# Cluster-match rows turned as 4-byte pairs, three zero matmuls fewer, and one attention block left in its place

## The chip, the cores and the metric

The kernel runs on one core of a Trainium2 chip. The metric is device time in microseconds (us) of one execution. PE is the matmul engine, ACT the engine that evaluates exponentials and other functions, DVE the vector engine, POOL the general-purpose engine, SP the engine that here only issues transfers (DMAs).

## The reference

Attention in which a query sees only the keys of its own cluster, followed by a gated feed-forward layer (FFN). There are 4 batches, 8 heads, 768 tokens, head size 64, and 16 cluster centroids per head.

```
q_n, k_n, c_n = rows of q, k, centroids divided by their norms
q_assign = argmax(q_n . c_n);  k_assign = argmax(k_n . c_n)      # 16 clusters
scores = where(q_assign == k_assign, scale * q k^T, -1e9)
attn = softmax(scores);  x = attn v            # heads side by side: 3072 x 512
out = (sigmoid(x w_gate) * (x w_val)) w_out     # 512 -> 1536 -> 512
```

## The kernel before, in words

**Units.** Two heads make a pair `p` (four pairs); the 768 queries of a head are halved (`qb` 0 and 1). A block is one batch, one query half and one pair. The list `blocks` holds 32 of them, ordered by batch, half, pair, except that line 256 takes the fifth, (batch 0, half 1, pair 0), and inserts it as the second. A block has six steps. A step is two score matmuls (line 911, 128 keys x 384 queries each, into the PSUM tile `sc`, of which there are two), one exponential on ACT over 128x768 (line 930, `es`), and six value matmuls (line 950) that add up in `av`, the only buffer of its kind. After the sixth step DVE takes reciprocals of the sums (line 988) and scales (line 991). The result is transposed into `x`, by a DMA (line 1014) or by PE and a DVE copy (lines 999 and 1010).

**The mask.** Nothing is masked by a select. Each key and each query gets 16 additional rows, a one where the token's cluster is and zeros elsewhere, weighted so that the product of two equal rows adds a large constant, which the bias of the exponential takes off again. The score matmul therefore contracts over 64+16 = 80 rows. The tiles `even` and `odd` hold the two operands (`NM`: k in 0, q in 1) for even and odd 128-token chunks. For query half 0 the q operand is the one in `even`, for half 1 the one in `odd`.

**Making the rows.** PE multiplies centroids and transposed k and q (lines 854, 734 for batch 0; 588 later) into a `ring` buffer: 32 rows (two heads x 16 clusters) by 384 tokens for each of four combinations. DVE then runs four operations: a transpose in 32x32 blocks into `t1`, so that clusters lie along the free dimension (lines 873, 760, 615); a maximum over each 16 (876, 761, 620); a comparison with that maximum, giving fp16 ones and zeros (863, 750, 598); and a transpose back. In batch 0 the way back is `place` (line 663): six transposes of 32x384 per pair, in the order even k and q of the first half, odd k, even k and q of the second half, odd k, each read from `ohf` with an offset of 16 columns where odd is wanted. The odd q rows are copied from the even tile by one DMA of SP (`odd<-even`, issued at line 281). In the other batches the way back is one transpose of 128x384 (line 608) into `oht`, from which eight DMAs of SP copy 16 rows each into `even` and `odd`.

**The FFN.** `feed` starts when all four pairs of a query half are in `x`: twelve times four gate matmuls, four value matmuls (line 1049), a tanh on ACT (1065) and a product on DVE (1076), and then 36 output matmuls (1096), an ACT scaling (1111) and the store.

**Order.** Every piece of work is a task with an engine, an estimated duration, a due time and its dependencies. A list scheduler places each where it can start first by its own estimates (the smaller due time where two are within 0.02 us) and so writes the order of each engine's queue. On the chip each engine follows its queue strictly, and waits where the next one's inputs are missing. So a changed duration or block order moves instructions on all engines. SP's queue holds the loads of k and q (for part of batch 1, and for batches 2 and 3, in quarters of 96 KB), the transposes into `x`, the mask copies and the stores.

**Warming.** Line 305 issues six 128x512 matmuls on zeros at the start. Line 1176 issues six more, behind the transposes of pair 1 and ahead of the first score matmul.

Of the kernel before, what the change touches and what calls it, by code (L numbers as in the profile page):

```python
# [164 lines left out]
def kernel(  # L165
# [38 lines left out]
        "odd": ([96, 2, S], HP), "oht": ([128, S], HP),  # L204
        "ohf": ([128, QB + NCL], HP), "t1": ([128, QB], FP), "mx": ([128, QB // NCL], FP), "oh": ([128, QB], HP),
        "es": ([128, 2, QB], HP), "rr": ([128, 2 * QCH], FP),
# [47 lines left out]

    for at, of in ((1, 4),):
        blocks.insert(at, blocks.pop(of))
    JS = list(range(0, NCH, 2)) + list(range(1, NCH, 2))
# [219 lines left out]
    act_scaled = nc.scalar.mul  # L477

    def dve_scaled(to, of, by):
        nc.vector.tensor_scalar(to, of, by, None, ALU.mult)  # L480

    def prepare(b, grp, due, step, act=(), queues=("SP",), split=False):
# [98 lines left out]
        for half in range(2):  # L581
# [14 lines left out]
            def same(oh=oh, t1=t1, mx=mx):  # L596
                take(oh)
                nc.vector.tensor_tensor(
                    grouped(oh), grouped(t1),
                    mx.tile[:n].unsqueeze(2).to_broadcast([n, QB // NCL, NCL]), ALU.is_equal,  # L600
                )

# [3 lines left out]
            def back(cols=cols, oh=oh, half=half):  # L606
                t = oht.tile if half else take(oht)
                nc.vector.transpose(t[:n, cols], oh.tile[:n])

# [4 lines left out]
            a1 = od.add(  # L614
                "DVE", 0.53, lambda t1=t1, rg=rg: nc.vector.transpose(take(t1)[:n], rg.tile[:n, :QB]),
                [cl], due, acq=[t1], uses=[rg],
# [36 lines left out]
    def place(b, p, ohf, tiles, last, due, alloc, c):  # L653


        ev, od_ = aug[b, p]
        for n_, (e, nm, h) in enumerate(
            ((0, "k", 0), (0, "q", 0), (1, "k", 0), (0, "k", 1), (0, "q", 1), (1, "k", 1))
        ):
            g = tiles.index((nm, h))  # L660
            m = od.add(
                "DVE", 0.6,
                lambda g=g, e=e, nm=nm, h=h: nc.vector.transpose(  # L663
                    aug[b, p][e].tile[64:96, NM[nm], h * QB : (h + 1) * QB],
                    ohf.tile[32 * g : 32 * g + 32, 16 * e : 16 * e + QB],
                ),
                [last, *alloc], due + 0.3 * n_, uses=[ohf, aug[b, p][e]],
            )
            masked[b, p, e, nm, h] = [c[nm, e, h], m]

        m = dma(
            "SP", lambda: od_.tile[64:80, NM["q"], :], lambda: ev.tile[80:96, NM["q"], :], 0.1,
            [masked[b, p, 0, "q", h][1] for h in range(2)] + alloc, due + (20.0 if p else 2.0), uses=[ev, od_],
        )
        for h in range(2):
            masked[b, p, 1, "q", h] = [c["q", 1, h], m]

    def prepare_pair(b, p, due, step, act=("q",), direct=False):
# [66 lines left out]
        def same():  # L745
            if direct:
                nc.vector.memset(take(oh)[:, QB:], 0.0)
            else:
                take(oh)
            nc.vector.tensor_tensor(  # L750
                grouped(oh), grouped(t1),
                mx.tile.unsqueeze(2).to_broadcast([128, QB // NCL, NCL]), ALU.is_equal,
            )

# [4 lines left out]
        for dur, go, acq, uses in (  # L759
            (0.61, lambda: nc.vector.transpose(take(t1), rg.tile[:, :QB]), t1, [rg]),  # L760
            (0.52, lambda: nc.vector.tensor_reduce(take(mx), grouped(t1), AX.X, ALU.max), mx, [t1]),
            (0.67, same, oh, [t1, mx]),
            (0.55, lambda: nc.vector.transpose(take(oht)[:, :QB], oh.tile), oht, [oh]),
        )[: 3 if direct else 4]:
            last = od.add("DVE", dur, go, [last], due, lat=0.0, acq=[acq], uses=uses)
# [24 lines left out]
    def prepare_first(due):  # L790
# [71 lines left out]
        def same():  # L862
            nc.vector.tensor_tensor(
                grouped(ohf), grouped(t1),
                mx.tile.unsqueeze(2).to_broadcast([128, QB // NCL, NCL]), ALU.is_equal,
            )

# [4 lines left out]
        for dur, go, acq, uses in (  # L872
            (0.58, lambda: nc.vector.transpose(take(t1), rg.tile[:, :QB]), t1, [rg]),
            (
                0.55,
                lambda: nc.vector.tensor_reduce(take(mx), grouped(t1), AX.X, ALU.max), mx, [t1],
            ),
            (0.6, same, None, [t1, mx, ohf]),
        ):
# [293 lines left out]
    def zeros_in_between():  # L1173
        ps = take(z_ring)
        for _ in range(6):
            nc.tensor.matmul(out=ps, lhsT=wz[:, 0:128], rhs=wz, start=True, stop=True)
# [38 lines left out]
```

## Time and profile before

| | |
|---|---|
| median of 3 runs | 328.13 us (327.52 to 328.47) |
| the profiled execution's own time | 327.7 us |
| its span | 325.9 us |
| busy: PE, ACT, DVE, POOL | 316.9, 227.8, 153.3, 64.6 us |
| six zero matmuls of line 1176 | 1.46 us, from 9.63 us on |
| first exponential | 11.69 us |
| first FFN matmul | 43.83 us |
| first output matmul of the FFN | 66.91 us |

A PE row's busy time counts each matmul from its start to its modelled end, and these overlap. A step's real pace is the distance between starts: four FFN matmuls of 128x384 take 0.65 us in the chain, so 0.163 us each, though the row says 325 ns. The granted TensorE clock is 1.00 in every stretch.

### The profile page before, as it was taken

The page shows a single profiled execution, that of the slowest core. Times are in us where ns is not written, and L with a number is a line of the kernel's source. Part 1 is how long each engine was busy: PE and PEld are TensorE (multiplying, and loading weights), DVE is VectorE, ACT ScalarE, POOL GpSimd, SP SyncE. Part 2 cuts the span into 40 slices and gives each one's busy share as a digit, 9 for nine tenths or more (in the row PEclk, how much of TensorE's full clock was granted, in tenths as well). Part 3 has the DMA queues.
Part 4 walks back from the last instruction along what each step waited for, and adds up shares of the span by engine and source line. Part 5 has one row for each costly group of instructions (what it writes and reads, how often), then busy time and mean ns, then how long its engine had stood idle before and what let it go on. Part 6 is the DMA issues. An engine that isn't in the chain of part 4 may idle for free.

```text
span 325.9 us, 7307 instructions
## 1 busy us (share of the span) xinstructions
PE 316.9 (97%) x2814; PEld 188.4 (58%) x2814; DVE 153.3 (47%) x332; ACT 227.8 (70%) x329; POOL 64.6 (20%) x109
## 2 busy tenths in 40 slices
PE   7988999999999999999999999999999999999995
PEld 4555756645666556565566555566566655654652
DVE  3989883546336329561264474742033311540430
ACT  5889958866797678776888677687788867332331
POOL 4997442130005313100024115000000000000000
PEclk9999999999999999999999999999999999999999
DMA  6999999736368884212867955210210012001002
GB/s 212 375 212 254 220 253 199 127 67 141 87 110 172 167 172 141 65 27 62 167 109 156 199 107 152 47 39 12 78 46 12 14 29 73 23 2 64 34 0 97
DMA packets 91522, 36.88 MB, mean 113 GB/s; under 512 B 76960, under 2 KB 86688, under 8 KB 91488
## 3 DMA queue, kind: packets, MB, share of 16 engines
q1 hardware_dynamic: 84960, 26.56, 36.3%
q0 software_dynamic: 6096, 9.44, 13.4%
q8 instruction: 22, 0.36, 0.5%
q10 hardware_dynamic: 432, 0.43, 0.4%
q14 instruction: 12, 0.10, 0.1%
HBM read 28.34 MB, written 6.29 MB: 106 GB/s over the span
## 4 chain that ended last, share of the span: by engine, by line
PE 88%; DVE 3%; DMA 3%; ACT 2%; SPq 1%; issue 1%; ACTq 0%; DVEq 0%
PE ring L1049 37%; PE ring L1096 19%; PE sc L911 17%; PE av L950 10%; PE ring L588 3%; ACT es L930 2%; DMA odd<-even 1%; SPq L281 1%; DVE even L663 1%; PE ring L517 1%; DMA cn<-in_centroids_dram 1%; DMA odd<-oht 1%; DVE odd L663 1%; ACT t L701 0%; PE ring L694 0%
## 5 line engine op out<-in xcount | busy, mean ns | idle before, releaser
L930 ACT ACTIVATE es<-sc,nbias 128x768 f16<-128x768 f32 x192 | 170.0, 902 | 45.1 <-PE sc L911 43.0
L1076 DVE SCALAR_TENSOR_TENSOR hT<-gt,ring 128x384 f16<-128x384 f32 x96 | 53.1, 553 | 102.4 <-PE ring L1049 95.6
L1049 PE MATMUL ring<-x,wv 128*128 128x384 f16 x384 | 78.1, 325 | 0.0
L1049 PE MATMUL ring<-x,wg 128*128 128x384 f16 x384 | 78.1, 326 | 0.0
L950 PEld LDWEIGHTS <-es 128*128 128x128 f16 x1152 | 58.3, 97 | 29.2 <-ACT es L930 2.5
L1096 PE MATMUL ring<-wo,hT 128*128 128x512 f16 x288 | 71.2, 379 | 0.0
L1065 ACT ACTIVATE gt<-ring 128x384 f32<-128x384 f32 x96 | 46.7, 487 | 32.1 <-DVE hT L1076 17.5
L950 PE MATMUL av<-vp,es 128*128 128x65 f16 x1152 | 64.9, 193 | 0.7 <-ACT es L930 0.7
L1049 PEld LDWEIGHTS <-wv 128*128 128x128 f16 x384 | 36.1, 97 | 22.8
L1049 PEld LDWEIGHTS <-wg 128*128 128x128 f16 x384 | 35.4, 97 | 22.8 <-issue 1.2
L550 POOL CAST even<-t 128x768 f16<-128x768 f32 x24 | 19.9, 828 | 105.1 <-PE av L950 33.3
L1096 PEld LDWEIGHTS <-hT 128*128 128x128 f16 x288 | 25.7, 98 | 25.5 <-issue 1.9
L911 PE MATMUL sc<-even 80*128 80x384 f16 x96 | 26.0, 326 | 1.3 <-ACT es L930 1.2
L911 PE MATMUL sc<-odd,even 80*128 80x384 f16 x96 | 26.2, 326 | 1.0 <-DMA odd<-even 1.0
L911 PE MATMUL sc<-even,odd 80*128 80x384 f16 x96 | 26.4, 325 | 0.4 <-DMA odd<-oht 0.2
L911 PE MATMUL sc<-odd 80*128 80x384 f16 x96 | 26.5, 325 | 0.0
L1111 ACT ACTIVATE osb<-ring 128x512 f32<-128x512 f32 x24 | 14.3, 597 | 14.3 <-PE ring L1096 13.5
L911 PEld LDWEIGHTS <-even 80*128 80x128 f16 x192 | 17.0, 98 | 12.5 <-issue 2.3
L911 PEld LDWEIGHTS <-odd 80*128 80x128 f16 x192 | 16.7, 99 | 10.2 <-issue 2.4
L453 POOL CAST vp<-nat 128x384 f16<-128x384 f32 x32 | 15.7, 521 | 29.2 <-DMA nat<-in_v_dram 24.3
L988 DVE RECIPROCAL rr<-av 128x6 f32<-128x6 f32 x32 | 6.1, 189 | 32.7 <-PE av L950 32.4
L498 DVE STREAM_TRANSPOSE t<-nat 128x384 f32<-128x384 f32 x40 | 20.7, 549 | 1.1 <-DMA nat<-in_q_dram 1.1
(78 smaller groups left out, 164.4 us busy)
## 6 DMA issues: line engine op xcount, KB each, us to landing
out_dram<-osb SPq DMA_DIRECT2D x24, 256.0 KB, 2.2
nat<-in_v_dram POOLq DMA_DIRECT2D x12, 384.0 KB, 5.2
nat<-in_k_dram SPq DMA_DIRECT2D x40, 96.0 KB, 3.6
nat<-in_q_dram SPq DMA_DIRECT2D x40, 96.0 KB, 3.4
odd<-even SPq DMA_DIRECT2D x12, 192.0 KB, 3.5
nat<-in_k_dram SPq DMA_DIRECT2D x5, 384.0 KB, 5.0
nat<-in_q_dram SPq DMA_DIRECT2D x5, 384.0 KB, 5.5
nat<-in_v_dram SPq DMA_DIRECT2D x4, 384.0 KB, 6.8
```

The source lines that it names most:

```text
L453: lambda e=e: nc.gpsimd.tensor_copy(vps[i % NVP][:, e, :, 0:D], buf.tile[:, e, :, :]),
L498: nc.vector.transpose(t[:, half * QB : (half + 1) * QB].rearrange("p (c x) -> p c x", x=128), blocks_[:, half],)
L550: nc.gpsimd.tensor_copy(t[:, NM[nm], cols], t32[p, nm].tile[:, cols])
L588: nc.tensor.matmul(out=ps[32 * g : 32 * g + 32, :QB], lhsT=cblk[:, 2 * p + half, :], rhs=t32[p, nm].tile[:, cols], start=True, stop=True,)
L911: nc.tensor.matmul(out=ps[:, i, :QB], lhsT=kb.tile[0:80, 0, e * QB + j // 2 * 128 : e * QB + (j // 2 + 1) * 128], rhs=qb_.tile[0:80, 1, e ...
L930: lambda: nc.scalar.activation(take(es), sc.tile[:, :, :QB], AF.Exp, bias=nbias, scale=D ** -0.5 if quarters(b, p) else scale,),
L950: nc.tensor.matmul(out=av.tile[:, g : g + D + 1], lhsT=es.tile[:, i, c * 128 : (c + 1) * 128], rhs=vp[:, e, j, :], start=first and i == 0 ...
L1049: nc.tensor.matmul(out=ps[:, :QB], lhsT=ws[fc // FPG][:, dcc, fc % FPG, :], rhs=xb.tile[:, dcc, :], start=(dcc == 0), stop=(dcc == NDC - 1),)
L1065: lambda rg=rg, gt=gt: nc.scalar.activation(take(gt), rg.tile[:, :QB], AF.Tanh, scale=0.5),
L1076: nc.vector.scalar_tensor_tensor(t[:, fc, :], gt.tile, 1.0, rv.tile[:, :QB], ALU.add, ALU.mult)
L1096: nc.tensor.matmul(out=ps, lhsT=hb.tile[:, fc, tb * 128 : (tb + 1) * 128], rhs=wos[fc // FPG][:, fc % FPG, :], start=(fc == 0), stop=(fc = ...
L1111: "ACT", 0.5, lambda rg=rg, osb=osb: nc.scalar.mul(take(osb), rg.tile, 0.5),
```

## The change

1. The match rows are written in another order. The transpose of the scores reads its input with stride 2, so that even and odd tokens of each 64 come to lie in two blocks of 32; the comparison (`matched`) writes its ones and zeros so that an even and an odd token's fp16 values are neighbours, 4 bytes together. The way back is then a transpose of half as many 4-byte elements (`turn_matches`): 32x192 in place of 32x384 in `place`, 128x192 in place of 128x384 at the former line 608. `ohf` is padded by 32 columns, not 16. The planner's estimates for these are 0.4 and 0.36 in place of 0.6 and 0.53 us.
2. Three zero matmuls ahead of the scores, not six.
3. Block (batch 0, half 1, pair 0) is not moved forward. Batch 0 runs the four pairs of half 0, then the four of half 1.

```
-        "ohf": ([128, QB + NCL], HP), ...
+        "ohf": ([128, QB + 2 * NCL], HP), ...
-    for at, of in ((1, 4),):
-        blocks.insert(at, blocks.pop(of))
+    def turn_scores(to, of):
+        nc.vector.transpose(
+            to.rearrange("p (b s c) -> p b s c", s=2, c=32),
+            of.rearrange("p (b i s) -> p b s i", s=2, i=32),
+        )
+    def matched(to, of, top):
+        nc.vector.tensor_tensor(
+            to.rearrange("p (b x s) -> p b s x", x=32, s=2).rearrange(
+                "p b s (g c) -> p b s g c", c=NCL
+            ),
+            of.rearrange("p (b s g c) -> p b s g c", s=2, g=2, c=NCL),
+            top.rearrange("p (b s g) -> p b s g", s=2, g=2).unsqueeze(4).to_broadcast(
+                [to.shape[0], QB // 64, 2, 2, NCL]
+            ),
+            ALU.is_equal,
+        )
+    def turn_matches(to, of):
+        nc.vector.transpose(to.bitcast(FP), of.bitcast(FP))
...
-                nc.vector.transpose(t[:n, cols], oh.tile[:n])
+                turn_matches(t[:n, cols], oh.tile[:n])
...
-                "DVE", 0.53, back, [a3], due, seq=turned[-1:],
+                "DVE", 0.36, back, [a3], due, seq=turned[-1:],
...
-                "DVE", 0.6,
-                lambda g=g, e=e, nm=nm, h=h: nc.vector.transpose(
+                "DVE", 0.4,
+                lambda g=g, e=e, nm=nm, h=h: turn_matches(
                     aug[b, p][e].tile[64:96, NM[nm], h * QB : (h + 1) * QB],
-                    ohf.tile[32 * g : 32 * g + 32, 16 * e : 16 * e + QB],
+                    ohf.tile[32 * g : 32 * g + 32, 32 * e : 32 * e + QB],
...
-        for _ in range(6):
+        for _ in range(3):
             nc.tensor.matmul(out=ps, lhsT=wz[:, 0:128], rhs=wz, start=True, stop=True)
-        "PE", 0.22 * 6, zeros_in_between, [], 1.0, seq=[last_turn[1], q0, c_cblk], acq=[z_ring]
+        "PE", 0.22 * 3, zeros_in_between, [], 1.0, seq=[last_turn[1], q0, c_cblk], acq=[z_ring]
```

All four transposes of scores (former lines 873, 760, 615) become `turn_scores`, all comparisons `matched`. In the orders that the scheduler writes, 70 score matmuls (35 steps) stood ahead of the first FFN matmul before, and 60 (30 steps) do now; value matmuls are 198 and 168. Ahead of the first output matmul all 96 score matmuls of batch 0 stand in both, and the scores of batch 1 begin after 4 output matmuls before, after 16 now. On SP's queue the first mask copy for batch 1 now stands ahead of the sixteen quarter loads, with five more behind them; before, all eight stood behind. The load of k for batch 1, pair 0, was issued before the first transpose into `x` and now comes behind it.

More of the change, by code (lines that the diff above doesn't have):

```diff
@@ L204 @@
         "odd": ([96, 2, S], HP), "oht": ([128, S], HP),
-        "ohf": ([128, QB + NCL], HP), "t1": ([128, QB], FP), "mx": ([128, QB // NCL], FP), "oh": ([128, QB], HP),
+        "ohf": ([128, QB + 2 * NCL], HP), "t1": ([128, QB], FP), "mx": ([128, QB // NCL], FP), "oh": ([128, QB], HP),
         "es": ([128, 2, QB], HP), "rr": ([128, 2 * QCH], FP),
@@ L597, in same @@
                 take(oh)
[L598 to L601, printed above, removed]
+                matched(oh.tile[:n], t1.tile[:n], mx.tile[:n])
             def weigh(oh=oh):
@@ L614, in prepare @@
             a1 = od.add(
-                "DVE", 0.53, lambda t1=t1, rg=rg: nc.vector.transpose(take(t1)[:n], rg.tile[:n, :QB]),
+                "DVE", 0.53, lambda t1=t1, rg=rg: turn_scores(take(t1)[:n], rg.tile[:n, :QB]),
                 [cl], due, acq=[t1], uses=[rg],
@@ L749, in same @@
                 take(oh)
[L750 to L753, printed above, removed]
+            matched(oh.tile[:, :QB], t1.tile, mx.tile)
         last = quad[p] = od.add(
@@ L759, in prepare_pair @@
         for dur, go, acq, uses in (
-            (0.61, lambda: nc.vector.transpose(take(t1), rg.tile[:, :QB]), t1, [rg]),
+            (0.61, lambda: turn_scores(take(t1), rg.tile[:, :QB]), t1, [rg]),
             (0.52, lambda: nc.vector.tensor_reduce(take(mx), grouped(t1), AX.X, ALU.max), mx, [t1]),
             (0.67, same, oh, [t1, mx]),
-            (0.55, lambda: nc.vector.transpose(take(oht)[:, :QB], oh.tile), oht, [oh]),
+            (0.55, lambda: turn_matches(take(oht)[:, :QB], oh.tile), oht, [oh]),
         )[: 3 if direct else 4]:
@@ L862, in same @@
         def same():
[L863 to L866, printed above, removed]
+            matched(ohf.tile[:, :QB], t1.tile, mx.tile)
         last = scored_ = od.add(
@@ L872, in prepare_first @@
         for dur, go, acq, uses in (
-            (0.58, lambda: nc.vector.transpose(take(t1), rg.tile[:, :QB]), t1, [rg]),
+            (0.58, lambda: turn_scores(take(t1), rg.tile[:, :QB]), t1, [rg]),
             (
```

## The prediction

> **What bounds the kernel now.** I read the busy table first, then busy time by stretches, because the share over the span mixes stages.
>
> ```profile
> PE 316.9 (97%) x2814; PEld 188.4 (58%) x2814; DVE 153.3 (47%) x332; ACT 227.8 (70%) x329; POOL 64.6 (20%) x109
> ...
> 10.00:24.00 14.00, 12.78 (x142) 8.00 (x143) 12.80 (x26) 11.45 (x18) 13.15 (x20) 1.00 1.13 283
> 24.00:44.00 20.00, 18.62 (x232) 12.07 (x225) 18.39 (x39) 18.20 (x23) 13.10 (x19) 1.00 1.20 242
> ...
> 65.00:70.00 5.00, 4.57 (x39) 2.44 (x38) 3.82 (x9) 2.64 (x5) 2.45 (x3) 1.00 0.27 52
> ...
> 100.00:110.00 10.00, 9.56 (x89) 5.27 (x88) 6.48 (x14) 6.54 (x9) 3.30 (x6) 1.00 0.90 191
> 110.00:314.00 204.00, 204.00 (x1775) 121.01 (x1774) 82.09 (x173) 141.15 (x206) 20.45 (x32) 1.00 0.33 76
> ```
>
> The columns after the length are PE, weight loads, DVE, ACT, POOL, clock, DMA. From 110 to 314 us PE never rests: there the time is PE's work and nothing else, and what the change saves on DVE is covered. Time can be won or lost where PE rests: before 44 us, and 0.43 and 0.44 us in the two stretches at 65 and 100. Before 44 us PE's rest is larger than its row shows, as the modelled ends of matmuls overlap. There DVE is busy 12.80 of 14 us, and ACT 18.20 of 20: first the masks from DVE, then the exponentials on ACT set the pace. So I next read the instructions in time and the chain of waits there.
>
> ```profile
> 9.25 0.56 DVE L863 TENSOR_TENSOR ohf<-t,mx 128x384 f16<-128x384 f32 x1
> 9.63 1.46 PE L1176 MATMUL av<-wz 128*128 128x512 f16 x6
> 9.85 1.17 DVE L663 STREAM_TRANSPOSE even<-ohf 32x384 f16<-32x384 f16 x2
> ...
> 11.16 0.65 PE L911 MATMUL sc<-even 80*128 80x384 f16 x3
> 11.69 1.69 ACT L930 ACTIVATE es<-sc,nbias 128x768 f16<-128x768 f32 x2 [1.25 <-PE sc L911]
> ...
> 17.35 0.50 PE L911 MATMUL sc<-odd,even 80*128 80x384 f16 x2 [1.02 <-DMA odd<-even]
> ...
> 27.76 11.76 ACT L930 ACTIVATE es<-sc,nbias 128x768 f16<-128x768 f32 x14 [0.20 <-PE av L950]
> ...
> 43.83 0.81 PE L1049 MATMUL ring<-x,wg 128*128 128x384 f16 x4
> ```
>
> The first scores start 0.14 us behind the second mask transpose (11.02), not behind the zeros (11.09). The early block of half 1 costs a wait for a DMA at 17.35. From 27.76 on exponentials follow each other at 11.76/14 = 0.84 us. The first FFN matmul comes at 43.83, when 35 steps of attention stand ahead of it. A step needs 2 x 0.163 + 0.185 = 0.51 us of PE (starts of score matmuls, and of value groups, in the chain), so PE is fed only once FFN work lies beside the steps.
>
> **The change, part by part.**
>
> *Narrower transposes.* The trace has no 192-column transpose. Its rows:
>
> ```profile
> L498 DVE STREAM_TRANSPOSE t<-nat 128x384 f32<-128x384 f32 x40 | 20.7, 549 | 1.1 <-DMA nat<-in_q_dram 1.1
> L663 DVE STREAM_TRANSPOSE even<-ohf 32x384 f16<-32x384 f16 x16 | 9.1, 570 | 0.5
> L608 DVE STREAM_TRANSPOSE oht<-oh 128x384 f16<-128x384 f16 x12 | 6.9, 576 | 0.3
> L337 DVE TENSOR_TENSOR csq<-cn 128x64 f32<-128x64 f32 x1 | 0.2, 226 | 1.7 <-DMA cn<-in_centroids_dram 1.7
> ```
>
> 4-byte and 2-byte elements cost the same (549 against 570 ns), so columns count. Two DVE products, 64 columns in 226 and 384 in 557 ns, give 1.03 ns a column; 192 fewer save 0.20 us, so 0.37. Ends: 0.57 (nothing saved) and 0.285 (half). I take 0.37, as it rests on two rows of like work. 24 transposes in the first 34 us save 4.8 us of DVE; twelve behind save 2.4 us under a PE that is full. [...]
>
> *Strided scores and comparison.* Reads with stride 2 in the transpose (now 0.58) and writes with stride 2 in the comparison (0.56) have no row; a strided one could cost double at worst, and nothing makes it shorter. I take unchanged, because the rows go by columns alone. Doubled, each pair pays 1.1 us, which the six transposes' 1.2 us outweigh.
>
> *Three zeros fewer.* 3 x 0.216 = 0.65 us of PE (starts of the row at line 1176), but the scores wait for DVE at 10.62 and the three that stay end near 10.4: nothing for itself. If that cover goes, 0.4 us.
>
> *Block order, and where steps then run.* First transposes at 9.85: two by 0.37 and the gap of 0.03 end at 10.62, scores at 10.76, first exponential 11.29 (11.69 before). Six steps, as before 5.14 us: 16.4. Step 7 is now pair 1. On DVE its scores are turned at 12.35; transpose, maximum, padding, comparison with gaps 1.8 us; then, in the new order, copy, copy, even k, copy, even q (3 x 0.51 + 2 x 0.37 + gaps): 16.6. ACT meanwhile takes two copies (0.47 each) that stand ahead of step 7: 17.4, against 17.95 before. Step 11 needs odd k of the second half, which stands behind pair 2's first two transposes. Two copies' and norms' 1.3 us, four transposes, pair 2's 1.8 us and three more transposes put it near 22.1, step 11 at 22.4, and step 12 ends near 24.1 (24.3 before). From there 0.84 us a step. Pairs 2 and 3 are ready near 21.6 and 27, ahead of their steps at 24.1 and 29.2.
>
> FFN: `x` needs step 24 (34.2) plus the reciprocals, scaling and transpose; DVE's order sets mask work of batch 1 ahead of the copy: 37.8. On PE step 30's scores stand ahead, which need the buffer of step 28 (24.1 + 16 x 0.84 = 37.5); with two value groups the FFN begins near 38.4. That is 5.4 us sooner, with five steps less done, 10 x 0.163 + 5 x 0.185 = 2.55 us. All else ahead of it is the same, so the first output matmul moves by -5.4 + 2.55 = **-2.9 us**, to 64.0.
>
> *SP's queue.* In batch 1 the first scores come after 16 output matmuls, 16 x 0.216 = 3.45 us, at 67.45; the odd-chunk score at 67.9. Its mask row:
>
> ```profile
> 64.25 3.25 SPq L281 DMA_DIRECT2D even<-oht x4
> 67.55 2.49 SPq L281 DMA_DIRECT2D odd<-oht x4
> ...
> 69.49 0.34 PE L911 MATMUL sc<-even,odd 80*128 80x384 f16 x1 [0.19 <-DMA odd<-oht]
> ```
>
> Sixteen quarter loads hold SP from 42.1 to 64.25. In the new order one mask copy stands ahead of them and waits for DVE's second transpose back, near 41, so loads start near 41.7; transfers bound them (the DMA engines are full to 55), and I leave their end at 64.2. The odd k row is the fourth copy behind: issued at 66.7, landed 1.9 later, 68.6: PE waits 0.7 where it waited 0.43: **+0.3**. At 100 to 110 PE rested 0.44 and would come 2.6 us sooner; between 0 and 0.44 more, I take **+0.2**. The load of k for pair 0 of batch 1, issued at 13.56 before and behind the first transpose now (20.4), lands at median 6.4 by 26.8; PE's turn of it stands at 26.1, with 0.84 us of exponential queued: nothing, at worst 0.7.
>
> Sum: -2.9 + 0.3 + 0.2 = **-2.4 us**. The profiled execution, 325.9 of span and 1.8 around it, is 327.7, 0.4 below the median 328.13; I forecast 325.3 for one like it and **325.7** against the median.
>
> **The rivals.** (1) *The transposes stay at 0.57.* Element size might set the pace, though 549 and 570 ns speak against it. Step 11 then waits for nine more times 0.20 us, the FFN begins at 40.2, and the gain is 0.6: 327.5. (2) *Slower: SP's head.* The mask copy set ahead of the loads blocks the queue until DVE's second transpose back; that needs PE's second batch-1 cluster product, and those need late k and q. If loads end at T, the odd row lands at T + 4.4 and PE needs it at 67.9; a loss begins where this wait passes the 2.9 won plus 0.43, at T = 66.8. Starting at 46 instead of 42.1 gives T = 68.1 and 1.4 us lost: 329.5. For it: SP has no rest from 42 to 64. Against: my 41 for the transpose. (3) *PE falls to half pace.* The six zeros at the start take 2.74/6 = 0.46 each, those of line 1176 0.216, with clock 1.00 in both rows: PE has a slow state that the clock column hides. Fewer zeros could bring it back for some us around 11 to 14, where PE works about 0.6 of the time: 2 us more, of which some 1.5 reach the steps: 327.2. [...]
>
> **How the numbers follow.** Forecast 0.58, (1) 0.18, (2) 0.16, (3) 0.08. About 0.3%, 1.0 us, is what measurement can tell from no change. Faster: the forecast, a third of (1), two thirds of (3): 0.69. Same: most of (1): 0.14. Slower: 0.17. If the waits at 65 and 100 vanish and the FFN starts 0.5 sooner the time is 324.1; the other cases but (2) reach 328.2. Range 324.2 to 328.4.
>
> **What would show it.** Mask transposes near 0.37 us; first exponential near 11.3; no `odd<-even` wait at 17; first FFN matmul near 38.4 and first output matmul near 64.0; PE full from 110 on as before. I am wrong if pair 1's masks hold step 7 beyond 18, if the FFN starts after 40, if a PE wait for `even<-oht` or `odd<-oht` passes 1.5 us near 67, or if matmuls after 10 us start 0.32 us apart.

## The result, and the profile after

The changed kernel takes **330.41 us** (median, 327.57 to 332.97), the kernel before beside it 328.07 us (326.74 to 330.66). The ratio is 1.0054 with a 95% interval of 1.0031 to 1.0077: about half a per cent slower, where 325.7 us was forecast. The ratios and intervals here and below leave out every execution more than 1.5% above the fastest of its kernel, so they are not quotients of the medians, which count all. The profiled execution shown here is the slowest of the twenty, 332.97 us with a span of 331.2 us, and its numbers are set against the 325.9 us span of before; a second one, nearer to the fast end, follows as e9.

First the two things that the change does by itself. DVE's groups in the profile after (count, then busy us, mean ns, idle time ahead):

```profile
L479 DVE STREAM_TRANSPOSE t<-ring 128x384 f32<-128x384 f32 x16 | 9.3, 580 | 18.9 <-PE ring L610 17.4 <-PE ring L870 1.2 <-PE ring L753 0.3
L486 DVE TENSOR_TENSOR oh<-t,mx 128x384 f16<-128x384 f32 x12 | 7.1, 589 | 0.3
L499 DVE STREAM_TRANSPOSE even<-ohf 32x192 f32<-32x192 f32 x16 | 5.9, 370 | 0.5
L499 DVE STREAM_TRANSPOSE oht<-oh 128x192 f32<-128x192 f32 x12 | 4.5, 377 | 0.3
L486 DVE TENSOR_TENSOR ohf<-t,mx 128x384 f16<-128x384 f32 x4 | 3.7, 926 | 0.1
```

The narrow transposes take 370 and 377 ns where the wide ones took 570 and 576. The strided transpose of the scores costs nothing (580 ns, 0.58 us before) and the strided comparison 0.03 us (589 ns in the other batches, 556 before). PE's instructions in time after (start, us, engine, line, what is computed, count, and in brackets the rest ahead and what ended it):

```profile
39.63 0.81 PE L1062 MATMUL ring<-x,wg 128*128 128x384 f16 x4
...
65.20 3.62 PE L1109 MATMUL ring<-wo,hT 128*128 128x512 f16 x16
72.44 0.65 PE L924 MATMUL sc<-even 80*128 80x384 f16 x3 [3.62 <-DMA even<-oht]
73.89 0.50 PE L924 MATMUL sc<-even,odd 80*128 80x384 f16 x1 [0.81 <-DMA odd<-oht]
74.19 1.91 PE L1109 MATMUL ring<-wo,hT 128*128 128x512 f16 x4
```

The first FFN matmul is 4.20 us sooner than before (43.83), the first output matmul 1.71 us sooner (66.91). All of that and more is lost directly behind: batch 1's first scores wait 3.62 us for the mask rows in `even`, and one step on 0.81 us for those in `odd`. The last line shows a second loss: four output matmuls take 1.91 us, where before they took 1.03:

```profile
66.91 1.03 PE L1096 MATMUL ring<-wo,hT 128*128 128x512 f16 x4
```

Busy time by stretches after (length, PE, weight loads, DVE, ACT, POOL, granted clock, DMA share, GB/s):

```profile
70.00:72.00 2.00, 0.00 (x0) 0.00 (x0) 1.04 (x2) 0.00 (x0) 0.58 (x1) 1.00 0.72 120
72.00:73.00 1.00, 0.56 (x3) 0.22 (x3) 0.76 (x2) 0.00 (x0) 0.25 (x1) 1.00 0.17 42
73.00:74.00 1.00, 0.19 (x2) 0.11 (x2) 0.28 (x1) 0.90 (x1) 0.65 (x1) 0.55 0.18 42
74.00:76.00 2.00, 2.00 (x5) 0.47 (x4) 0.00 (x0) 0.90 (x1) 0.17 (x1) 0.50 0.30 64
76.00:78.00 2.00, 2.00 (x16) 0.67 (x16) 0.31 (x1) 0.00 (x0) 0.00 (x0) 0.50 0.30 63
78.00:80.00 2.00, 2.00 (x12) 1.08 (x11) 1.86 (x5) 1.21 (x2) 0.00 (x0) 0.52 0.81 228
80.00:82.00 2.00, 2.00 (x23) 0.72 (x21) 0.25 (x1) 1.87 (x3) 0.00 (x0) 1.00 0.37 103
```

Behind the rest the clock granted to PE is half from about 73.1 to 79.95, 6.85 us, which by estimate (half of 6.85) does 3.4 us less work. So the sum against before is: -1.7 (first output matmul), +4.2 (waits of 3.62 and 0.81 less the 0.19 for `odd` before), +3.4 (half clock), -0.4 (the rest at 100 to 110 is gone), +0.3 (a rest past 110): +5.8, and the spans differ by 5.3; the half microsecond between them is not accounted for.

Why the rows are late is read from SP's queue after (each line is the time from issue to the queue's next one):

```profile
41.33 0.54 SPq L279 DMA_DIRECT2D even<-oht  x1
41.96 0.70 SPq L279 DMA_DIRECT2D nat<-in_k_dram  x1
...
43.45 5.02 SPq L1027 DMA_TRANSPOSE x<-xn  x1
...
63.41 2.35 SPq L1027 DMA_TRANSPOSE x<-xn  x1
...
67.81 2.14 SPq L279 DMA_DIRECT2D nat<-in_q_dram  x3
70.00 1.91 SPq L279 DMA_DIRECT2D even<-oht  x3
71.96 1.22 SPq L279 DMA_DIRECT2D odd<-oht  x2
```

The sixteen loads begin at 41.96, as before (42.10), and end at 69.95 instead of 64.25. Two transposes into `x` now stand among them and hold the queue for 5.02 and 2.35 us; before, one stood there and held it 1.46 us:

```profile
61.42 1.46 SPq L1014 DMA_TRANSPOSE x<-xn  x1
62.92 1.29 SPq L281 DMA_DIRECT2D nat<-in_q_dram  x2
64.25 3.25 SPq L281 DMA_DIRECT2D even<-oht  x4
```

The difference, 5.9 us, is about what the loads end later here; in e9 below it is 5.6, and the loads end only 3.2 us later, so a hold is not simply added to the end. Seven mask copies follow the loads, not the five that the section on the change counts: five, a transpose, and two.

### The profile page after: what moved, and what is told of

The parts are those of the page before. It is cut to its first block, busy times and chain, and to the rows that moved or that the text cites. A ratio compares the mean times of both kernels' runs of the same rounds, so it can differ in the third digit from the quotient of the medians.

```text
span 331.2 us, 7314 instructions
## 1 busy us (share of the span) xinstructions
PE 318.4 (96%) x2811; PEld 189.0 (57%) x2811; DVE 148.3 (45%) x332; ACT 228.3 (69%) x329; POOL 64.9 (20%) x109
## 4 chain that ended last, share of the span: by engine, by line
PE 86%; SPq 5%; DVE 3%; POOL 1%; ACT 1%; issue 1%; DMA 1%; DVEq 0%
PE ring L1062 35%; PE ring L1109 18%; PE sc L924 17%; PE av L963 10%; SPq L279 5%; PE ring L610 3%; DVE even L499 1%; PE av L303 1%; PE ring L539 1%; SPq L1027 1%; POOL odd L838 1%; ACT es L943 1%; DVE t L502 1%; POOL even L838 1%; DMA odd<-oht 1%
## 5 line engine op out<-in xcount | busy, mean ns | idle before, releaser
L963 PEld LDWEIGHTS <-es 128*128 128x128 f16 x1152 | 59.0, 98 | 30.3 <-issue 2.4
L963 PE MATMUL av<-vp,es 128*128 128x65 f16 x1152 | 65.6, 194 | 0.9 <-ACT es L943 0.9
L1062 PEld LDWEIGHTS <-wg 128*128 128x128 f16 x384 | 35.1, 97 | 22.2 <-issue 1.2
```

What stands on the lines that cost most here:

```text
L963: nc.tensor.matmul(out=av.tile[:, g : g + D + 1], lhsT=es.tile[:, i, c * 128 : (c + 1) * 128], rhs=vp[:, e, j, :], start=first and i == 0 ...
L1062: nc.tensor.matmul(out=ps[:, :QB], lhsT=ws[fc // FPG][:, dcc, fc % FPG, :], rhs=xb.tile[:, dcc, :], start=(dcc == 0), stop=(dcc == NDC - 1),)
```

## The experiments

Medians and ratios to the kernel before, which ran beside each group of experiments (its medians were 327.84 to 329.04). The last column counts the executions whose mean granted clock was at least 0.997. The kernel before itself reaches that in 22 of 35, 19 of 35, 18 of 35, 10 of 23 and 18 of 23; in the rest its mean is mostly 0.99 to 0.995, as much as one or two stretches at half clock of the 3.4 us seen in e2, e7, e9 and e10 would take (3.4 x 0.5 / 328 = 0.005, an estimate).

| experiment | median us | ratio, 95% interval | full clock |
|---|---|---|---|
| the changed kernel | 330.41 | 1.0054, 1.0031 to 1.0077 | 2 of 20 |
| e9, again | 331.65 | 1.0047, 1.0009 to 1.0085 | 1 of 12 |
| e1, loads later | 327.04 | 0.9953, 0.9925 to 0.9981 | 9 of 12 |
| e2, 14 zeros in the rest | 329.61 | 1.0048, 1.0023 to 1.0074 | 9 of 12 |
| e8, 22 zeros in the rest | 330.17 | 1.0050, 1.0019 to 1.0080 | 9 of 12 |
| e3, weights sooner | 331.02 | 1.0059, 1.0024 to 1.0094 | 1 of 12 |
| e14, output weights late | 328.81 | 1.0001, 0.9962 to 1.0040 | 6 of 13 |
| e13, transposes on PE | 326.13 | 0.9922, 0.9892 to 0.9952 | 10 of 12 |
| e15, before, transpose on PE | 327.69 | 1.0005, 0.9973 to 1.0037 | 8 of 12 |
| e16, e13 with six zeros | 326.07 | 0.9942, 0.9915 to 0.9969 | 10 of 12 |
| e4, block order alone | 329.14 | 1.0035, 1.0009 to 1.0061 | 10 of 12 |
| e6, pairs alone | 328.34 | 0.9998, 0.9967 to 1.0030 | 8 of 12 |
| e7, three zeros alone | 328.46 | 0.9991, 0.9962 to 1.0021 | 8 of 12 |
| e5, pairs and three zeros | 328.31 | 0.9990, 0.9962 to 1.0017 | 7 of 12 |
| e10, before, masks first | 328.05 | 0.9977, 0.9950 to 1.0004 | 6 of 12 |
| e11, pairs, masks first | 327.52 | 0.9976, 0.9949 to 1.0003 | 8 of 12 |
| e12, e1 with six zeros | 327.08 | 0.9946, 0.9918 to 0.9974 | 11 of 12 |

### Is it the wait for the mask rows?

**e1** lets the second group of quarter loads be due at 48, not 42. The scheduler then puts all eight mask copies ahead of them.

```
-                            due - 60 if b else 42 if grp[0] else 20,
+                            due - 60 if b else 48 if grp[0] else 20,
```

> Edit: in the changed kernel the sixteen quarter loads of k and q for pairs 2 and 3 of batch 1 may start at 48, not 42, of the planner's time, so that all eight mask copies for pairs 0 and 1 stand ahead of them on SP's queue. Theory A (the mask copies wait behind the loads, PE rests 4.4 us for them near 70 us, and after the rest its clock is halved for 6 us): copies issued by 50, no PE wait for oht rows above 0.5 us between 60 and 80, granted clock 1.00 throughout, first output matmul near 65, time 326 to 327.5, some 3 to 4 us below the changed kernel. Rival B (the clock falls for another cause, the zeros that were removed or the order of the blocks): the clock still falls below 1.00 between 65 and 85 and the time stays above 329. Rival C (the loads, now later, are late for pairs 2 and 3): a new PE wait near 85 to 95, time 328 to 330.

The first FFN matmul came at 39.66, the first output matmul at 65.56 with four score matmuls already done ahead of it; no wait for mask rows was left. In its stretches PE is nearly full and the clock is whole:

```profile
65.00:70.00 5.00, 5.00 (x41) 2.71 (x41) 3.02 (x7) 3.08 (x4) 1.34 (x3) 1.00 0.77 127
70.00:75.00 5.00, 4.49 (x34) 1.74 (x32) 2.74 (x5) 1.91 (x3) 1.36 (x2) 1.00 0.60 144
75.00:80.00 5.00, 5.00 (x46) 2.51 (x44) 3.52 (x10) 3.27 (x5) 0.00 (x0) 1.00 0.33 94
```

One date on SP's queue turns a loss of 0.5% into a gain of 0.5%. The loss is the wait, and what hangs on it.

**e9** is the changed kernel once more, for a second profiled execution.

> The changed kernel once more, on the same chip and against the same runs of the kernel before as the next three. Theory (wait for the mask rows of batch 1, then the half clock): median 329.5 to 330.8, ratio 1.004 to 1.007; most executions with a mean granted clock of 0.995 or less, where most of the kernel before have 1.00; in the profile the loads end at 66 to 70, PE waits 2 to 4 us for even<-oht, and the clock near 75 is 0.5 to 0.8. If it falls into an execution with clock 1.00, the wait is under 2.5 us. Rival (the loss is spread over the whole span): PE's rest beyond 80 us as large as near 70.

Its profiled execution (329.16 us, span 327.4) is on the fast side of its median of 331.65, as the first was on the slow side. It shows the same places, smaller: loads end at 67.4, the two transposes hold SP 5.75 and 1.28 us, PE waits 1.55 us for `even` and 0.68 for `odd`, and the half clock lasts 3.4 us, from 72.55 to 75.95. Beyond 80 us PE rests 0.25 us in all, so the loss is not spread.

### What does the half clock cost by itself?

**e2** and **e8** put matmuls on zeros, 14 and 22, behind the sixteen output matmuls, so that PE works while it waits.

```
+    wo_tasks = []
...
+                wo_tasks.append(prev[0])
...
+    w_ring2 = Buf("av")
+
+    def keep_warm():
+        ps = take(w_ring2)
+        for _ in range(14):      # e8: 22
+            nc.tensor.matmul(out=ps, lhsT=wz[:, 0:128], rhs=wz, start=True, stop=True)
+    z2 = od.add("PE", 0.01, keep_warm, [exps[47]], 1.0, seq=[wo_tasks[3]], acq=[w_ring2])
+    od.behind(scored_last[96], [z2])
```

> Edit: in the changed kernel 14 matmuls on zeros (14 x 0.216 = 3.0 us) stand between the first 16 output matmuls and the first scores of batch 1, just where PE rested 3.6 us. Theory A: the scores start no later, as they wait for the mask copies anyhow (near 72.4), but the clock stays 1.00 behind them, so the 6 us at half clock, some 3 us of work, are won: time 327 to 328.5. Rival B (clock falls for another cause): clock still 0.5 behind 73, time 330 to 333. Rival D (PE's rest alone costs, the clock nothing on the path): clock 1.00 and the time still within 1 us of the changed kernel's 330.4.

Fourteen zeros left rests of 0.82 and 0.71 us ahead of the scores, which began at 72.63 as without them. The clock still fell, for 3.4 us (74.5 to 77.9), half as long: the span was 330.0. So two rests that add up to 1.5 us were enough.

> The changed kernel with 22 zero matmuls (4.75 us at 0.216 each) behind the 16 output matmuls and ahead of batch 1's first scores, at 68.7, so that PE works until about 73.5; fourteen had ended at 71.7 and left 1.5 us of rest. Theory A (about 4 us of the changed kernel's loss are rest and about 3 us the half clock behind the rest): scores at 73.5 to 74 as in the changed kernel, clock 1.00 throughout, span about 3 us below the 331.2 of the changed kernel's profiled execution, 327.5 to 328.7. Rival (the low clock has another cause than PE's rest, so that it comes all the same): clock near 0.5 for 3 to 6 us behind 73, 329.5 to 331.

With 22 the scores began at 72.96, half a microsecond later than in the changed kernel, and yet the span was 327.9, 3.3 us shorter. Its stretches at the same place:

```profile
72.00:74.00 2.00, 2.00 (x12) 0.96 (x10) 0.88 (x2) 0.45 (x1) 0.83 (x1) 1.00 0.16 39
74.00:76.00 2.00, 2.00 (x24) 0.77 (x23) 0.46 (x1) 1.24 (x2) 0.00 (x0) 1.00 0.32 67
76.00:78.00 2.00, 2.00 (x25) 1.07 (x26) 1.86 (x5) 1.87 (x3) 0.00 (x0) 1.00 0.36 78
78.00:80.00 2.00, 2.00 (x20) 0.78 (x15) 1.24 (x3) 1.69 (x3) 0.00 (x0) 1.00 0.92 263
```

From the first score matmul that reads `odd` (73.45 here, 73.89 there) to the end of the span it took 2.9 us less, and this leaves out both waits. The half clock by itself is thus worth some 3 us of that execution, a little less than the 3.4 us worked out above. The median hardly gains; the likely reason, which one profile can't show, is that the zeros hold the scores back to 73 also in executions where the rows land sooner. Over all executions the clock's part is smaller: the 12 of e9 take 331.0 us on average with a mean clock of 0.9929, the 35 of the kernel before beside them 328.6 with 0.9973. Span times missing clock is 2.3 and 0.9 us. Of the difference of 2.4 us, 1.4 is clock and the other 0.9 is the wait less what was won.

### Why did the loads end late?

Two causes were open: the two transposes among the loads, and the traffic of POOL's queue. There the last output weight is issued sooner than before (36.73 us, 39.04 before), but POOL waits for the last of v until 60.67 us, where it was 55.29. **e3** lets the third weight load be due at 20, not 22, which moves it ahead of the casts of pair 3.

```
-    WT = (14, 16, 22, 24, 27, 30, 33, 36, 39)
+    WT = (14, 16, 20, 24, 27, 30, 33, 36, 39)
```

> Edit: in the changed kernel the third weight load's planned time is 20, not 22, which puts it and the weight loads behind it ahead of POOL's casts for pair 3, as before the change. Theory A1 (the loads of batch 1 end at 70.0 and not at 64.2 because weight and v transfers, 4 us later, share the DMA engines until 57, not 51): weight transfers end near 53, the sixteen loads near 65 to 66, PE's wait for mask rows under 2 us though all eight copies stand behind the loads here, time 327.5 to 329. Theory A2 (the two transposes into x that stand among the loads hold SP by themselves): loads end near 69 to 70 still, PE waits 4 us or more, time 330 or above.

The loads ended at 66.7, but then came a third transpose and all eight mask copies (the scheduler had moved the first one behind), and PE waited 2.1 and 1.2 us with one stretch at half clock. As e9 has its loads end at 67.4 without any such edit, 66.7 shows nothing on the weights.

**e14** lets the output weights be due at 53, 56 and 59, behind four loads of v.

```
-    WT = (14, 16, 22, 24, 27, 30, 33, 36, 39)
+    WT = (14, 16, 22, 24, 27, 30, 53, 56, 59)
```

> The changed kernel with the three loads of the output weights due at 53, 56 and 59 instead of 33, 36 and 39, behind four loads of v on POOL's queue; two transposes and one mask copy stay among and ahead of the sixteen loads. Theory W (weight traffic): the first loads of the group pass sooner, the one transpose holds SP 1.2 to 2.5 instead of 5.0 us, loads end at 62 to 66, a wait under 1.5 us, 327.5 to 329. Theory T (the transposes hold the queue by themselves): loads end at 67 to 70, waits of 1.5 to 3.5 us, 329.5 to 331. If the output weights then come too late, PE waits for wo at 65 to 68, and the run says nothing on either.

It does not settle the question, but the first half of its loads speaks for the weights. Without the output weights beside them, ten loads and a transpose were through by 54 us, 12.4 us after the first load; in the changed kernel four loads and a transpose took 11.3 us. In the second half the late weights stand beside the loads. Its SP queue, DVE and PE (the profiled execution is the slowest of its thirteen) show that, and what a late load does further on:

```profile
43.06 2.85 SPq L1027 DMA_TRANSPOSE x<-xn  x1
...
47.33 3.43 SPq L279 DMA_DIRECT2D nat<-in_k_dram  x3
...
54.08 6.00 SPq L1027 DMA_TRANSPOSE x<-xn  x1
...
65.18 1.04 DVE L520 STREAM_TRANSPOSE t<-nat 128x384 f32<-128x384 f32 x2 [9.85 <-DMA nat<-in_q_dram]
...
66.71 1.44 PE L1062 MATMUL ring<-x,wg 128*128 128x384 f16 x4 [8.45 <-DVE hT L1089]
```

A quarter of q, late, stood ahead of the FFN's products in DVE's strict order, and PE waited 8.45 us for `hT`. The same transfer held the queue for 5.02 us at 43 in the changed kernel and for 2.85 us here, and the second one for 2.35 and 6.00 us: the hold is no fixed cost of the transfer (e3 had one of 1.19 us at 42).

**e13** takes the two transposes off SP: PE and a DVE copy make them, as elsewhere in the kernel. Mask copies, loads and weights keep their order.

```
-        if not ((b, qb) == (0, 0) and p >= 2 or slot >= NS - 2):
+        if not ((b, qb) == (0, 0) and p >= 2 or (b, qb) == (0, 1) and p < 2 or slot >= NS - 2):
```

> The changed kernel with the transposes into x of batch 0, half 1, pairs 0 and 1 made by PE and a DVE copy instead of a DMA on SP's queue; mask copies, loads and weights keep their order (one mask copy ahead of the sixteen loads, three and four behind). Theory T (the two transposes among the loads hold the queue): with their 5 to 7 us gone and no transfer in their place, the loads end at 63 to 66, even<-oht at 66 to 69 lands ahead of PE's need at 69, PE waits under 1 us for oht rows, clock 1.00 near 75, and 327 to 328.5 (PE and DVE pay 2 x 0.3 and 2 x 0.56 us for the transposes). Theory W (the DMA engines are full with weights, so that a load waits as long without the transposes): loads end at 66.5 to 69.5, waits of 1.5 to 3.5 us, 329.5 to 331.

SP's queue in it:

```profile
43.09 2.87 SPq L279 DMA_DIRECT2D nat<-in_k_dram  x1
46.05 4.89 SPq L279 DMA_DIRECT2D nat<-in_q_dram  x1
50.99 5.78 SPq L279 DMA_DIRECT2D nat<-in_k_dram  x3
...
60.98 2.11 SPq L279 DMA_DIRECT2D nat<-in_q_dram  x3
63.14 2.98 SPq L279 DMA_DIRECT2D even<-oht  x3
66.16 2.49 SPq L279 DMA_DIRECT2D odd<-oht  x4
```

The loads end at 63.1. PE's only wait for mask rows is 0.62 us at 68.18, the clock is 1.00, and the span is 324.1: 1.8 us less than before. The weights kept their order and nearly their times, so taking the two transposes away is enough, and they were the cause. That does not clear the weights, under whose traffic they stood (e14). Nor is a hold the price of a transpose: in the place of the first one, at 43.09, a load now holds the queue for 2.87 us, and the next one for 4.89. The price is read from the length of the sixteen loads, which is 28.0 us in the changed kernel's profile, 25.8 in e9 and 21.5 here: 2.2 to 3.2 us for each of the two. e13 is also the fastest version here, with e16.

**e15** is the control: the same edit on the kernel before, for the one transpose that stands among its loads.

```
-        if not ((b, qb) == (0, 0) and p >= 2 or slot >= NS - 2):
+        if not ((b, qb) == (0, 0) and p >= 2 or (b, qb) == (0, 1) and p == 1 or slot >= NS - 2):
```

> The kernel before with the one transpose that stands among its sixteen quarter loads (batch 0, half 1, pair 1) made by PE and a DVE copy; all else on SP keeps its order. Theory (the gain of the version without transposes is the change's own): the loads end 1 to 2 us sooner than 64.25, but PE waited only 0.19 us for odd<-oht and rested 0.43 between 65 and 70, so at most 0.4 is won, less 0.3 for PE's transpose: 327.5 to 328.5, ratio 0.997 to 1.002. Rival (the transposes' way pays in either kernel): ratio 0.995 or below.

Its loads end at 63.3 instead of 64.25, in 20.7 us instead of 22.2, and nothing is won. So what e13 wins is the change's own gain, set free.

### The parts of the change, one by one

**e4** is the kernel before with the block order alone (part 3), **e6** the pair transposes alone (part 1, with the new estimates), **e7** the three zeros alone (part 2), **e5** parts 1 and 2.

```
e4, on before:
-    for at, of in ((1, 4),):
-        blocks.insert(at, blocks.pop(of))
e5, on the changed kernel: the same two lines put back
e6: as e5, and range(6), 0.22 * 6 for the zeros
e7, on before:
-        for _ in range(6):
+        for _ in range(3):
-        "PE", 0.22 * 6, zeros_in_between, ...
+        "PE", 0.22 * 3, zeros_in_between, ...
```

> Edit: the kernel before with the block order of the changed one (half 1 of pair 0 not moved forward) and nothing else; transposes of 384 columns, six zeros. If the block order alone brings the late masks: FFN starts near 41, PE waits 2 to 5 us for mask rows of batch 1 near 70, clock drop behind it, time 329 to 333. If the narrow transposes and the slower comparison (0.93 us in batch 0, not 0.56) are what harms: no such wait, time 327 to 328.5, like before.

> The kernel before with the pair transposes, the strided comparison and the new estimates alone; six zeros, the second half moved forward. No mask copy stands ahead of the sixteen loads. Theory A: loads begin near 41 and end near 64 to 65 as before, the fourth odd row lands 4.4 later, near 69, and PE, whose first FFN matmul comes at 42 to 42.8 (43.83 before) with as many steps done, needs it at 66.5 to 67: a wait of 1.5 to 2.5 us, which gives back all of the 1 to 1.8 won: 327.5 to 329. The prediction's own sum, with the masks free, would give 326.5 to 327. Theory B (blocks cost, pairs pay): 326.5 to 327 and no wait for oht above 0.5 us.

> The kernel before with three zeros, not six, ahead of the first scores, and nothing else; only PE's planned times differ. The prediction says nothing for itself: first scores at 11.0 to 11.2, 327.8 to 328.6, that is within 0.3% of before. Rival (PE falls to half pace for want of work around 11 to 14): matmuls behind 11 us start 0.32 us apart, not 0.16, the first FFN matmul comes 1 to 2 us later than 43.83, and 329 to 330.

> The changed kernel with the block of pair 0's second half moved forward again, as before the change; narrow transposes and three zeros stay. Theory A (the loss is the order on SP's queue, where a mask copy that waits for DVE stands ahead of the sixteen quarter loads, and PE's rest behind it lowers the clock): that mask copy is ahead of the loads here too, with the other three and the four odd ones behind them, so I expect the loads to begin at the copy's issue near 41 and to end at 65 to 67, a wait of PE for even<-oht or odd<-oht of 1 to 3 us near 68 to 72, and 327.5 to 329.5, with a clock below 1.00 near 70 to 77 if the rest passes 2 us. First FFN matmul 42 to 42.8, with 35 steps done. Theory B (it is the order of the blocks that costs, not the masks): no wait for oht above 0.5 us, first FFN matmul 42 to 42.8, and 326 to 327.

The first FFN matmul and the first output matmul of the profiled executions tell the parts apart:

| | first FFN matmul | first output matmul |
|---|---|---|
| before | 43.83 | 66.91 |
| e6, pairs | 44.35 | 67.36 |
| e7, three zeros | 45.84 | 68.92 |
| e5, pairs, three zeros | 43.27 | 66.29 |
| e4, block order | 42.43 | 69.78 |
| the changed kernel | 39.63 | 65.20 |

The pair transposes alone win nothing: in the old order step 7 waits 1.1 us for the copy `odd<-even`, which DVE's speed does not bring (17.60 against 17.35 before). Nor did e6 wait for mask rows of batch 1, as its first theory had it. The block order alone loses 2.9 us at the first output matmul: the FFN starts 1.4 us sooner, but with five steps and two cluster products of batch 1 (sixteen matmuls, 1.7 us) less done. Neither expectation for e4 was met: batch 1's first scores waited only 0.94 us, for a cast of `even` on POOL, the clock stayed at 1.00, and the kernel was slower all the same. Together the parts win 1.7, some 5 us more than the sum of the two; as e4's profiled execution is 1.5 us above its median, part of the 5 us can be that execution's own. The exponentials of e4 show what the wide transposes do in the new order (ACT in time):

```profile
19.68 0.90 ACT L928 ACTIVATE es<-sc,nbias 128x768 f16<-128x768 f32 x1
...
25.66 10.21 ACT L928 ACTIVATE es<-sc,nbias 128x768 f16<-128x768 f32 x12 [1.82 <-PE sc L909]
```

Step 7 runs at 19.68 and the steady row of exponentials begins at 25.66, against 17.43 and 22.96 in the changed kernel (the row begins with step 10 there and with step 11 here). In the new order the masks of pairs 0 and 1 come off DVE just ahead of the steps that need them, and there narrow transposes count. e5 differs from the changed kernel by the block order alone. Its mask copy also stands ahead of the loads, which shows that this by itself does little: waits of 0.19 and 0.70 us. One transpose stands among its loads, as before the change, and two in e4, as in the changed kernel: the block order is what brings the second. Its first FFN matmul came at 43.27, later than either theory had it.

e7 shows a half clock in another place. Ahead of step 7, PE waited 1.55 us for `odd<-even`, and from 17.8 to 21.2 the clock was half, so that the FFN came 2.0 us late; at full clock its executions take 327.9 us on average, as those of the kernel before (327.7). That need not be owed to the zeros, as **e10** shows: the kernel before, six zeros and all, with loads due at 52, so that all masks stand ahead of them.

```
-                            due - 60 if b else 42 if grp[0] else 20,
+                            due - 60 if b else 52 if grp[0] else 20,
```

> The kernel before with the second group of quarter loads due at 52 instead of 42, so that all eight mask copies of batch 1 stand ahead of them, as in the experiment on the changed kernel with 48. It is the control for that one. If what the changed kernel with later loads wins over the kernel before (0.9 us at clock 1.00) is the change's own gain, the kernel before must not win here: it waits only 0.19 us for odd<-oht, so 327.6 to 328.6, ratio 0.998 to 1.002. Rival (putting the masks first pays by itself): ratio below 0.997. If the loads then come too late for the cluster products of batch 1, a wait for nat<-in_k or t appears at 70 to 80 and the time is above 329.

Stretches of its profiled execution:

```profile
16.00:18.00 2.00, 0.32 (x3) 0.08 (x1) 1.84 (x4) 0.83 (x2) 1.44 (x4) 1.00 1.14 340
18.00:20.00 2.00, 1.82 (x22) 1.55 (x23) 0.71 (x3) 1.23 (x2) 1.94 (x4) 0.91 1.21 202
20.00:22.00 2.00, 2.00 (x9) 1.24 (x8) 1.69 (x3) 1.85 (x4) 1.88 (x3) 0.50 1.24 206
22.00:24.00 2.00, 2.00 (x21) 0.67 (x20) 0.45 (x1) 1.32 (x3) 1.50 (x3) 0.74 0.95 153
```

Here the wait for `odd<-even` was 1.9 us and the half clock came from 19.65 to 23.05. Putting the masks first is worth at most little in the kernel before: the interval holds 1, and at full clock its executions take 327.1 us on average against 327.6, where e1 took 326.8 against 327.8. Some of what e1 wins may thus not be the change's own. It is worth about as little in **e11**, which is e6 with loads due at 48, though its first FFN matmul was no sooner (44.80).

> Part one alone (narrow transposes, six zeros, second half of pair 0 moved forward) with the loads due at 48, so that all eight mask copies stand ahead of them. In the run of part one alone the first FFN matmul came at 44.35 (43.83 in the kernel before) and no wait for masks was above 0.2. If narrow transposes gain nothing without the new order of blocks, this is 327.3 to 328.5, ratio 0.997 to 1.002, first FFN matmul 43.5 to 44.5. Rival (their gain is hidden in the masks' wait): ratio below 0.997.

**e12** (e1 with six zeros) and **e16** (e13 with six zeros) undo part 2 where no wait hides it.

```
-        for _ in range(3):
+        for _ in range(6):
-        "PE", 0.22 * 3, zeros_in_between, ...
+        "PE", 0.22 * 6, zeros_in_between, ...
```

> The changed kernel with the loads due at 48 and with six zeros ahead of the first scores, not three: it undoes part two in the version that is free of the wait for masks (327.04, ratio 0.9953 with three zeros). Theory (zeros are worth nothing but what PE rests ahead of the first scores): the scores start at 10.8 to 11.1 instead of 10.4 to 10.7, because six zeros end near 11.0; a step later everything is as with three; 327.0 to 327.6, ratio 0.995 to 0.998. Rival (zeros keep the clock up behind 14 us): fewer executions below clock 0.997 and 326.5 to 327.

> The changed kernel without the two transposes among the loads (326.13, ratio 0.9922 with three zeros), and with six zeros: part two undone where no wait for masks hides it. If three zeros are worth nothing, 325.8 to 326.6 and a ratio of 0.991 to 0.994; if they bring the first scores forward by 0.3 us and this reaches the end, 326.3 to 326.8, ratio 0.993 to 0.995; if six keep the clock up behind the start, fewer executions below a mean clock of 0.997 than 2 of 12, and 325.5 to 326.

Both agree with their three-zero versions within the intervals (327.08 and 327.04; 326.07 and 326.13). No worth of the zeros is seen either way; 11 and 10 of 12 executions at full clock against 9 and 10 do not show more.

## Why the prediction was wrong, step by step

**Narrower transposes: right.** 0.37 was taken, 0.370 to 0.377 measured. Half of 0.57 would be 0.285; the measurement decides for the estimate from the two DVE products (226 ns for 64 columns, 557 for 384), which has a fixed part of some 160 ns. Strided access was taken as free: the scores' transpose has 0.58 us as before, the comparison 0.03 us more, and no run shows the doubled time that stood as the worst case. What the "nothing" missed is that the four comparisons of batch 0 took 0.93 us on average. The run with the old comparison, e4, also had two at 0.75 and 1.18 us, so it is not the stride alone. In the profile after the second, third and fourth took 1.14, 0.88 and 1.10 us, each beside a cast on POOL (the last from 25.31 to 26.41, the cast from 25.15 to 25.98). But the first, 0.60 us from 8.81 on, ran beside casts too (8.45 to 9.75), and so did one of 0.56 us in the profile before (from 14.66, casts from 14.70 on). That the casts slow them is thus not shown.

**Zeros: right**, by e7, e12 and e16. Rival (3), half pace around 11 to 14 for want of zeros, did not occur: in the profile after, the three score matmuls from 10.36 on start 0.16 us apart. Nor did rival (1), as the transposes did not stay at 0.57.

**Block order: right in sign, 1.2 us too large.** -2.9 was forecast for the first output matmul, -1.71 came (-2.05 in e9, -1.74 in e13). In the profile shown, step 11 ran at 22.96, not 22.4 (22.61 in e9), behind comparisons of 1.14 and 0.88 us for pairs 1 and 2 where before they took 0.56; the sixteen steps from there took 0.854 us each and not 0.84, 0.2 in all; and one further wait of 0.49 us for scores stood at 37.1. Together that is the 1.2 us by which the FFN began later than 38.4. The wait for `odd<-even` at 17 vanished as forecast, and so did the rest at 100 to 110 (forecast +0.2, came -0.4).

**SP's queue: the step that failed.** It said "transfers bound them (the DMA engines are full to 55), and I leave their end at 64.2" and made +0.3 of it. The end was 69.95 in the profile shown and 67.4 in e9, and the term came out at +4.2 and, in e9, +2.0 us (1.55 and 0.68 less 0.19). The count of what stands on the queue was taken for mask copies and loads, and not for the transposes into `x`: the other block order moved these too, from one to two among the loads, and e13 puts their price at 2.2 to 3.2 us each on the end of the loads. Rival (2) had the place, the rule "if loads end at T, the odd row lands at T + 4.4", and the point from which it decides (T = 66.8), but looked for the delay at the head of the queue. The head was on time (41.33, loads from 41.96), and the delay was in the middle.

**The clock: not in the sum at all.** The sign named for being wrong, a wait for `even<-oht` or `odd<-oht` above 1.5 us near 67, is what came. But the wait was priced at its own length; here rests of 2.2 us (e9) and 4.4 us (the profile shown) were followed by 3.4 and 6.85 us at half clock, some 1.7 and 3.4 us more. The prediction asked after PE's pace for the zeros at the start alone, in rival (3), and not for the wait that its own rival (2) put at 68.

With the transposes out of the way part of the forecast comes true: e13's span is 1.8 us below that of before, where -2.4 was forecast. That its median of 326.13 stands beside the forecast 325.7 is partly luck: at full clock its executions take 326.1 us on average and those of the kernel before beside it 327.45, 1.35 us less.

## What to carry to other kernels

When an edit moves work in time, recount everything that its new order puts on each shared transfer queue, transposes and stores too, and ask for each how long it holds the queue under the traffic of its new place (1.2 to 6.0 us for a transpose here). Price a new rest of the matmul engine at its length plus, once rests close together add up to about 1.5 us, the slow stretch that may follow them (3.4 us at 0.50 behind 0.82 and 0.71 us in e2, none behind 1.6 us in e11). A faster operation pays only where it sets the pace: try it with the order it was meant for, as neither part here won anything alone.

## What the runs showed of the hardware that was not expected

- Short rests were followed by a lower clock; in e8, which had none there, it stayed at 1.00. Rests of 0.82 and 0.71 us (e2), of 1.55 us (e7), of 1.55 and 0.68 us (e9) and of 2.06 and 1.22 us (e3) were each followed by one stretch of 3.4 us at 0.50, as was one of 1.9 us in e10 and in e12; in the changed kernel's profile 3.62 and 0.81 us by 6.85 us, twice that. In e16 no rest but the one at the start was longer than 0.7 us, and PE was busy 12.61 of the 14 us from 10 to 24, and yet the mean clock from 24 to 44 us was 0.83, as much as 6.8 us at half. Rests of 0.19 and 0.70 us (e5) were not followed by a slow stretch, nor were one of 1.6 us in e11 and one of 1.5 us in e15. So no single length is the edge, and the 2 us that e5's expectation names was an estimate: rests of 1.53 us in all within 2.2 us were enough in e2, and one of 1.6 us was not in e11. The fall comes 1.6 (e7) to 4.3 us (the changed kernel) after the rest begins.
- The kernel before pays this too. 13 to 17 of its 35 executions have a mean clock below 0.997, and at full clock it takes 327.6 to 327.8 us on average, against 329.5 to 329.7 in the others. In e7 and e10 the place was the wait for `odd<-even` ahead of step 7. That it is the same place in the kernel before is likely, but its profile is of an execution at full clock.
- A DMA transpose among loads held SP's queue from 1.2 (e3) to 6.0 us (e14), but a load in the same place held it for 2.87 us (e13): the hold is no price. Two transposes less shortened the stretch of the sixteen loads by 4.3 to 6.5 us (e13).
